# Magnitudes of every odd unit on ScalarE, the second layer one tick later, and x requested right behind its last reader

## The chip, the cores and the metric

The kernel runs on one core of a Trainium2 chip. Its engines are TensorE (PE, with its weight loads PEld), VectorE (DVE), ScalarE (ACT), GpSimd (POOL) and SyncE (SP, which here only issues DMAs). The metric is device time in microseconds (us) of one execution.

## The reference

Two stages follow each other. The attention has 4 batches of 12480 tokens with 128 channels and 32 inducing vectors; the second stage is a layer of width 2048 with a rational activation between its two matmuls.

```python
def mab(q, kv):
    s = scale * (q @ kv.transpose(0, 2, 1))
    s = s - s.max(-1, keepdims=True)
    a = np.exp(s)
    a /= a.sum(-1, keepdims=True) + 1e-09
    return a @ kv
h = mab(I, x)          # 32 inducing rows over all tokens of a batch
x = mab(x, h)          # every token over the 32 rows of h

h = x @ w_in           # (49920, 128) @ (128, 2048)
P = a[0] + a[1] * h + a[2] * h2 + a[3] * h3
Q = 1.0 + np.abs(b[0]) * np.abs(h) + np.abs(b[1]) * h2
g = P / (Q + 1e-06)
return (g @ w_out).astype(np.float32)
```

## The kernel before

**Units and ticks.** A batch is cut into 26 token tiles of 480 tokens. The first layer's 2048 columns are cut into 8 pairs of 128. One pair over one tile is a *unit*, with the key (b, n, q): batch, tile, and pair q from 0 to 7. There are 4 x 26 x 8 = 832 units, and a tile is eight of them. `fast_ticks` (line 894) issues one unit after the other, a *tick* each. Every engine takes its own instructions in the order in which they are written there, since the order is pinned. The engines run apart from each other and wait only for data and for buffers to come free.

**A unit's way.** `first` (838) makes the unit's 128x960 hidden values in PSUM with two f16 matmuls (`hp<-at,st`) a tick ahead; three such buffers `hp` exist. The unit's magnitudes `u` are taken one of two ways:

- A *plain* unit has `mask` (904) on VectorE, which reads `hp` and clears the sign bit (`DVE TENSOR_SCALAR u<-hp`). Then `moved` (853) adds a constant to `hp` with two further matmuls on TensorE (`hp<-same,by`), so they have to wait for the mask.
- A *shifted* unit has the constant already in `hp`, and one `Abs` with a bias on ScalarE (`ACT ACTIVATE u<-hp,all`) undoes it on the way. It needs no `moved`.

`shifted` (778) says which is which: of the odd q, 1, 3 and 7 are shifted and 5 is plain, and the even q are all plain. One tick later VectorE makes `l` of `u` and `hp` (`l<-u,all,hp`), which releases `hp`. Two units share one tile of `u`, and ScalarE turns each such pair with one `Ln` and, four ticks on, one `Sigmoid` (128x1920 each; a table load stands ahead of each run of four). Thirteen ticks behind a unit's first tick (`BEHIND`), in odd ticks, VectorE finishes the even unit of a pair (`l<-l,all,u`) and POOL the odd one with two instructions (`last_on_pool`, 952). `second` (858) then multiplies by `w_out` and adds up the 16 column blocks of a tile in `po`, of which there is one buffer. It comes fourteen ticks behind the unit.

**The end of a tile.** With q = 7, `second` adds two bf16 matmuls (`po<-at,st`), and the tile's sums are then complete. The next call of `fetch` (879) copies them with VectorE (`oT<-po`) and requests the write to `out` on SP. That call is the one in `side` (789), at the end of the same tick. A tick whose `second` has q = 0 is called *late*: its `second` stands at the tick's end, since it needs `po` to be copied away. Fourteen ticks behind, the tile's end falls into the tick of the unit q = 5, and the late tick is that of q = 6. The engines' order at that place is

```
tick q=5  PE:  second(q=7) first half, first(q=6), second(q=7) second half, bf16 pair, moved(q=5)
          DVE: finish, mask(q=5), l of q=4, side: copy of po
tick q=6  PE:  first(q=7), moved(q=6), side, second(q=0)
          DVE: mask(q=6), l of q=5, side
```

**Attention as side work.** `side` hands out pieces of the attention to the ticks, by budgets for TensorE, VectorE and POOL. `ahead` (740) works on the next batch: `pass1` (375) scores it against the inducing vectors, `pooled` (446) adds its values up, then the new first-layer weights are made. `attend` (767) works on the batch at hand: `pass3` (651) scores tokens against the 32 rows of `HT`, and `spread` (723) sends the results to the tiles `at` with four small DMAs per 480 tokens. The last batch has no `ahead`.

**How x comes in.** All DMAs stand in SP's one queue, in program order: x by columns for `pass1` (`xTa<-x_c`) and `pass3` (`xTb<-x_c`), x by rows for `pooled` (`x<-x_t`, with a POOL memset beside it), the `at<-hl` pieces and the `out<-oT` writes. Each kind of x has four buffers, a block of 480 tokens in each. `columns` (333) requests block n + 4 when block n + 1 is taken, and `pooled` requests block n + 3 ahead of the matmuls of block n. Blocks are used in groups of four, so the fourth block of a group is requested in the step that uses it. `landed` (327) holds a group back until three ticks after the request of its fourth block, if that request is already made.

Of the kernel before, what the change touches and what calls it, by code (L numbers as in the profile page):

```python
# [21 lines left out]
M = 32  # L22
C = 128
HB = 4
BT = HB * TP
# [167 lines left out]
class Kernel:  # L193
# [138 lines left out]

    def columns(self, b, kind):

        ts = [self.x_columns(b, n, kind) for n in range(4)]

        def turns():
            for n in range(self.NB):
                yield ts.pop(0)
                if n + 4 < self.NB:  # L340
                    ts.append(self.x_columns(b, n + 4, kind))

        return turns()

    def wide_columns(self, b):

# [28 lines left out]
    def pass1(self, b):  # L375

        nc, ap = self.nc, self.ap
        X = mybir.AxisListType.X
        e = ap.tile([P, self.NG, BT], F32, tag="e", name=f"e{b}")
        mxs = ap.tile([P, self.NG, 2], F32, tag="mxs", name=f"mxs{b}")  # L380
        nc.gpsimd.memset(mxs, -3.0e38)
        xs = self.wide_columns(b) if self.boot else self.cols.pop((b, "a"))
        for g in range(self.NG):
            nb = min(4, self.NB - 4 * g)
            yield from self.landed("a", b, g)
            yield "pe", 1.0
            pc = self.misc(f"pc{b}_{g}")
            for j in range(nb):
                nc.tensor.matmul(pc[M * j:M * j + M, 0:BT], self.ind, next(xs), start=True, stop=True)
            rows = slice(0, M * nb)  # L390
            for i in range(2):
                yield "v", 0.36
                c = slice(BT // 2 * i, BT // 2 * (i + 1))
                nc.vector.tensor_scalar(out=e[rows, g, c], in0=pc[rows, c], scalar1=1.0, scalar2=None, op0=ALU.mult, op1=ALU.max, accum_out=mxs[rows, g, i:i + 1])
            self.free()
        if self.boot:
            self.wide_rows(b)
        else:
            self.xs[b] = [self.x_rows(b, n) for n in range(4)]
        yield "v", 0.1  # L400
        mx = ap.tile([P, 1], F32, tag="mx", name=f"mx{b}")
        nc.vector.tensor_reduce(out=mx, in_=mxs.rearrange("p g i -> p (g i)"), axis=X, op=ALU.max)
        yield "pe", 0.2
        pm = self.misc(f"pm{b}")
        nc.tensor.transpose(out=pm[0:1, 0:P], in_=mx, identity=self.ident)
        yield "v", 0.3
        mt = ap.tile([1, 1, M], F32, tag="mt", name=f"mt{b}")
        nc.vector.tensor_reduce(out=mt[:, 0], in_=pm[0:1, 0:P].rearrange("o (j m) -> o m j", m=M), axis=X, op=ALU.max)
        self.free()
        nm = ap.tile([1, 4, M], F32, tag="H", name=f"nm{b}")  # L410
        nc.vector.tensor_scalar(out=nm, in0=mt.broadcast_to((1, 4, M)), scalar1=-1.0 / math.sqrt(C), scalar2=None, op0=ALU.mult)
        yield "pe", 0.2
        pb = self.misc(f"pb{b}")
        nc.tensor.matmul(pb[:, 0:4], nm.rearrange("o j m -> o (j m)"), self.ones, start=True, stop=True)
        yield "v", 0.1
        nmc = ap.tile([P, 1], F32, tag="nmc", name=f"nmc{b}")
        nc.vector.tensor_copy(out=nmc, in_=pb[:, 0:1])
        self.free()
        self.e[b] = e
        self.exps.append(lambda: self.exp_rows(b, e, nmc))  # L420
        self.flush()
# [24 lines left out]
    def pooled(self, b, own=None):  # L446

        nc, ap = self.nc, self.ap
        e = self.e[b]
        acc = ap.tile([P, C + 1], F32, tag="acc", name=f"acc{b}")  # L450
        xs = self.xs.pop(b)

        def turned(g):
            rows = slice(0, M * min(4, self.NB - 4 * g))
            for c in range(HB):
                yield "pe", 0.22
                if c == 0:
                    pt = self.misc(f"pt{b}_{g}").rearrange("p (c n) -> p c n", c=HB)
                nc.tensor.transpose(out=pt[0:TP, c, rows], in_=e[rows, g, TP * c:TP * c + TP], identity=self.ident[rows, rows])
            eT = ap.tile([TP, HB, P], F32, tag="eT", name=f"eT{b}_{g}", bufs=2)  # L460
            yield from self.act(lambda: nc.scalar.activation(eT[:, :, rows], pt[0:TP, :, rows], AF.Identity, bias=0.0, scale=1.0))
            eTs.append(eT)

        eTs, early = [], int(self.boot)
        while self.e_done.get(b, 0) < self.NG:
            self.flush()
            yield "wait", 0
        if early:
            yield from turned(0)
        for g in range(self.NG):  # L470
            nb = min(4, self.NB - 4 * g)
            if g + early < self.NG:
                yield from turned(g + early)
            eT = eTs.pop(0)
            self.free()
            yield from self.landed("x", b, g)
            for k in range(HB * nb):
                j, c = divmod(k, HB)
                if c == 0:
                    yield "pe", 0.4  # L480
                if k == 0:
                    ph = self.misc(f"ph{b}_{g}")
                if c == 0 and self.boot and (4 * g + j) % 3 == 0 and g + j:
                    self.xs[b] = xs
                    self.wide_rows(b)
                elif c == 0 and not self.boot and 0 < 4 * g + j < self.NB - 3:
                    xs.append(self.x_rows(b, 4 * g + j + 3))
                nc.tensor.matmul(ph[M * c:M * c + M, 0:C + 1], eT[:, c, M * j:M * j + M], xs[4 * g + j][:, c, :], start=(j == 0), stop=(j == nb - 1))
            yield "v", 0.2
            if g == 0:  # L490
                nc.vector.tensor_copy(out=acc, in_=ph[:, 0:C + 1])
            else:
                nc.vector.tensor_tensor(out=acc, in0=ph[:, 0:C + 1], in1=acc, op=ALU.add)
            self.free()
        yield "pe", 0.3
        pq = self.misc(f"pq{b}")
        nc.tensor.matmul(pq[0:M, 0:C + 1], self.fold, acc, start=True, stop=True)
        yield "v", 0.4
        rs = ap.tile([M, 1], F32, tag="rs", name=f"rs{b}")
        nc.vector.tensor_scalar(out=rs, in0=pq[0:M, C:C + 1], scalar1=1e-9, scalar2=None, op0=ALU.add)  # L500
        nc.vector.reciprocal(out=rs, in_=rs)
        yield "v", 0.2
        H = ap.tile([M, C], F32, tag="H", name=f"H{b}")
        nc.vector.tensor_scalar(out=H, in0=pq[0:M, 0:C], scalar1=rs, scalar2=None, op0=ALU.mult)
        self.free()
        yield "pe", 0.3
        pt = self.misc(f"HT{b}")
        nc.tensor.matmul(pt[:, 0:4 * M], H, self.ident4.rearrange("p a m -> p (a m)"), start=True, stop=True)
        yield "v", 0.2
        while own is None and self.scored < b - 2:  # L510
            yield "wait", 0
        HT = own if own is not None else ap.tile([C, 4 * M], F32, tag="HT", name=f"HT{b}", bufs=2)
        nc.vector.tensor_copy(out=HT, in_=pt[:, 0:4 * M])
        self.free()
        self.HT[b] = HT
# [135 lines left out]
    def pass3(self, b, groups):  # L651
# [4 lines left out]
        for fours in groups:  # L656
            wide = ap.tile([TP, 2, HB, 4, M], F32, tag="a", name=f"a{b}_{fours[0]}")
            todo = []
            for i, r in enumerate(fours):
# [3 lines left out]
                for j in range(HB * nb):  # L663
# [1 line left out]
                    if j == 0:  # L665
                        pc = self.misc(f"pd{b}_{r}")
                    if j % HB == 0:
                        xT = next(self.cols[b, "b"])
                    nc.tensor.matmul(pc[0:TP, M * j:M * j + M], xT[:, TP * (j % HB):TP * (j % HB) + TP], self.HT[b][:, 0:M], start=True, stop=True)
                a = wide[:, i, :, 0:nb]  # L670
                sc = pc[0:TP, 0:HB * nb * M].rearrange("p (j c m) -> p j c m", m=M, c=HB)
                yield "v", 0.7
# [104 lines left out]

    def shifted(self, q):

        return self.fast and q % 2 == 1 and q != 5  # L780

    def step(self, which):

# [110 lines left out]
    def fast_ticks(self, units):  # L894
# [10 lines left out]
            V.tensor_scalar(out=u.u.bitcast(I32), in0=u.h.bitcast(I32), scalar1=0x7FFFFFFF, scalar2=None, op0=ALU.bitwise_and)  # L905

        self.first(units[0])
        for t in range(n + BEHIND + 2):
            u, last, d, done = at(t), at(t - 1), at(t - BEHIND), at(t - BEHIND - 1)
            group, turn = divmod(t - TURNS - 2, 2 * TURNS)  # L910
            w = at(2 * TURNS * group + 2 * (turn % TURNS))
            late = done and done.key[2] == 0
# [6 lines left out]
            if u:  # L919
                if t % 2 == 0:  # L920
                    u.pair = self.mp.tile([P, 2, 2, BT], F32, tag="u", name=f"u{u.i}", bufs=self.rooms["u"])
                    u.u = u.pair[:, 0]
                    mask(u)
                    if late:
                        self.fetched = self.fetch()
                else:
                    u.u = last.pair[:, 1]
                    if not plain(u):
                        A.activation(u.u, u.h, AF.Abs, bias=p.z_back, scale=1.0)
            if t % 2 and d:  # L930
                V.scalar_tensor_tensor(out=d.g, in0=d.g, scalar=p.z_k3, in1=d.u, op0=ALU.add, op1=ALU.mult)
                self.last_on_pool(at(t - BEHIND + 1), d)
# [11 lines left out]
                A.activation(w.pair, w.pair, AF.Sigmoid, bias=p.lnc, scale=-2.0)  # L944
            self.side(u or units[-1])
            if late:
                if not u:
                    self.fetch()
                self.second(done)
        self.fetch()  # L950

# [123 lines left out]
                self.again()  # L1075


class Unit:


# [26 lines left out]
```

## Time and profile before

| | |
|---|---|
| median of 3 runs | 2566.98 us (2561.35 to 2567.44) |
| the profiled execution, its own time | 2566.77 us |
| its span, first to last instruction | 2564.9 us |
| TensorE (PE) busy | 2285.1 us, 89% |
| VectorE (DVE) busy | 2269.3 us, 88% |
| ScalarE (ACT) busy | 2149.7 us, 84% |
| POOL busy | 1445.7 us, 56% |
| mean granted TensorE clock | 0.956 of 2.4 GHz |

The three engines that carry the units are all near nine tenths busy, but the shares are means over a stretch with much side work and one with little. 188.8 us pass ahead of the first copy of a finished tile, and the ticks of the tiles counted 0 to 61 lie beside the side work of two kinds until 1699.1 us. The remaining 42 tiles lie beside score passes alone. Matmul ends are modelled in these records, so start-to-start distances are used where they can be. An instruction's line is in most cases that of a helper (L177), so it is found by its tiles.

### The profile page before, as it was taken

To read this page: it belongs to the slowest core of one execution; us is meant where nothing else is said; L and a number is where in the kernel's file an instruction comes from. 1 tells how busy PE (TensorE), PEld (TensorE's weight loads), DVE (VectorE), ACT (ScalarE), POOL (GpSimd) and SP (SyncE) were. 2 spreads that over 40 slices of the span, in tenths; PEclk is the share of its full clock that TensorE was granted. 3 is DMA by queue.
4 is the path that set the end of the run, shared out by engine and by line. 5 is a ranking of instruction groups with operands and counts; after the bars stand their busy time and mean duration, and the time that the engine had idled before them with its cause. 6 is when DMAs were issued, how large, how long until landed. Compare 5 with 4: busy or idle time off the path is not lost.

```text
span 2564.9 us, 25969 instructions
## 1 busy us (share of the span) xinstructions
PE 2285.1 (89%) x8670; PEld 1112.6 (43%) x8670; DVE 2269.3 (88%) x2490; ACT 2149.7 (84%) x1487; POOL 1445.7 (56%) x997
## 2 busy tenths in 40 slices
PE   4479999899899899999889989999999999999997
PEld 2244444444434444444434434444444444444443
DVE  2688899889998988988798879999999999999995
ACT  1177899888888998988799968889989899999995
POOL 0325566555555565665465546565656566666666
PEclk6579999999999999999999989999999999999999
DMA  9113201310132012002211220001010100000000
GB/s 251 53 31 115 64 26 31 78 50 20 58 100 62 18 52 66 28 27 89 81 35 35 70 58 27 12 20 43 24 43 23 44 18 30 18 18 20 16 16 17
DMA packets 117112, 121.03 MB, mean 47 GB/s; under 512 B 13289, under 2 KB 115561, under 8 KB 116969
## 3 DMA queue, kind: packets, MB, share of 16 engines
q1 hardware_dynamic: 116969, 119.28, 16.4%
q8 instruction: 70, 1.15, 0.2%
q14 instruction: 73, 0.60, 0.1%
HBM read 80.89 MB, written 25.56 MB: 42 GB/s over the span
## 4 chain that ended last, share of the span: by engine, by line
PE 44%; DVE 33%; issue 11%; ACT 6%; DMA 3%; POOL 2%; SPq 1%; DVEq 0%; POOLq 0%; ACTq 0%
PE po L177 27%; DVE l L177 15%; DVE u L177 12%; PE hp L177 10%; ACT u L177 4%; PE pd L177 3%; DVE oT L177 2%; ACT L177 1%; DVE asm L177 1%; PE pc L177 1%; SPq L177 1%; POOL u L177 1%; DMA xw<-x_t 1%; DMA xTw<-x_c 1%; DVE cv L177 1%
## 5 line engine op out<-in xcount | busy, mean ns | idle before, releaser
L177 PE MATMUL po<-l,w_out 128*128 128x480 f32 x3328 | 1579.4, 580 | 9.0 <-POOL l L177 8.1
L177 DVE SCALAR_TENSOR_TENSOR l<-u,all,hp 128x960 f32<-128x960 f32 x832 | 1002.2, 1205 | 32.8 <-PE hp L177 21.8
L177 POOL TENSOR_SCALAR u<-l,all 128x960 f32<-128x960 f32 x416 | 447.3, 1075 | 958.9 <-DVE l L177 838.7
L177 POOL TENSOR_TENSOR l<-u 128x960 f32<-128x960 f32 x416 | 927.0, 2228 | 34.6
L177 PEld LDWEIGHTS po<-l,w_out 128*128 128x128 f32 x3328 | 628.9, 193 | 380.9 <-issue 213.2
L177 ACT ACTIVATE u<-u,all 128x1920 f32<-128x1920 f32 x416 | 765.3, 1887 | 1.2
L177 ACT ACTIVATE u<-u 128x1920 f32<-128x1920 f32 x416 | 737.5, 1797 | 5.6 <-DVE l L177 4.5
L177 DVE TENSOR_SCALAR u<-hp 128x960 int32<-128x960 int32 x520 | 597.2, 1148 | 99.1 <-PE hp L177 97.2
L177 ACT ACTIVATE u<-hp,all 128x960 f32<-128x960 f32 x312 | 328.0, 1051 | 263.2 <-PE hp L177 257.3
L177 DVE SCALAR_TENSOR_TENSOR l<-l,all,u 128x960 f32<-128x960 f32 x416 | 521.1, 1253 | 2.4 <-ACT u L177 2.4
L177 PE MATMUL hp<-at,st 128*128 128x480 f16 x1664 | 481.0, 371 | 21.3 <-DVE l L177 17.5
L177 PE MATMUL hp<-same,by 96*128 96x480 f16 x1040 | 302.3, 372 | 140.0 <-DVE u L177 134.0
L177 PEld LDWEIGHTS <-st 128*128 128x128 f16 x1872 | 183.0, 99 | 490.1 <-issue 475.1
L177 ACT ACT_TABLE_LOAD x235 | 301.5, 1283 | 4.8 <-PEq L1100 0.7
L177 PEld LDWEIGHTS <-by 96*128 96x128 f16 x1040 | 102.6, 99 | 369.9 <-issue 333.4
L177 DVE COPY oT<-po 128x480 f32<-128x480 f32 x104 | 67.8, 651 | 61.3 <-PE po L177 61.1
L177 PEld LDWEIGHTS pd<-HT,xTb 128*120 128x120 f32 x832 | 101.9, 195 | 17.0 <-issue 9.7
L177 PE MATMUL pd<-HT,xTb 128*120 128x32 f32 x832 | 98.7, 274 | 3.9 <-DMA xTb<-x_c 3.8
L177 PE MATMUL po<-at,st 128*128 128x480 f16 x208 | 59.1, 366 | 0.0
L177 DVE TENSOR_SCALAR_CACHE_REDUCE e<-pc 128x240 f32<-128x240 f32 (+1 forms) x56 | 21.1, 401 | 31.9 <-PE pc L177 31.9
L177 ACT ACTIVATE a<-a 120x512 f32<-120x512 f32 (+2 forms) x21 | 14.9, 728 | 41.1 <-DVE a L177 41.0
L177 PE MATMUL ph<-x,eT 120*32 120x129 f32 x624 | 25.6, 292 | 24.0 <-DMA x<-x_t 14.0
(110 smaller groups left out, 609.4 us busy)
## 6 DMA issues: line engine op xcount, KB each, us to landing
xTb<-x_c SPq DMA_DIRECT2D x104, 240.0 KB, 2.8
out<-oT SPq DMA_DIRECT2D x104, 240.0 KB, 2.0
xTa<-x_c SPq DMA_DIRECT2D x78, 240.0 KB, 3.0
x<-x_t SPq DMA_DIRECT2D x78, 240.0 KB, 4.0
at<-hl SPq DMA_DIRECT2D x416, 30.0 KB, 1.8
xw<-x_t SPq DMA_DIRECT2D x8, 720.0 KB, 13.1
xTw<-x_c SPq DMA_DIRECT2D x5, 960.0 KB, 12.4
raw<-w_in SPq DMA_DIRECT2D x4, 480.0 KB, 10.3
```

What stands on the lines that cost most here:

```text
L177: ins = call(*args, **kw)
```

## The change

Four edits are made together.

- `shifted` loses its exception: q = 5 is shifted too. In 104 units a mask on VectorE and two `moved` matmuls on TensorE go, and an `Abs` on ScalarE comes.
- `second` and what follows it come fifteen ticks behind a unit. The end of a tile falls into the tick of q = 6, and the late tick is that of q = 7. VectorE's and POOL's last steps stay thirteen ticks behind.
- The call of `fetch` in a late tick stands behind both branches, since late ticks are odd now. The call in `side` still comes first in all but the first ticks.
- The class `Blocks` replaces the generator of `columns`. Its `read`, called right behind the last matmul that reads a block, requests the next block. `pooled` does the same for x by rows: block n + 4 behind the last matmul of block n, with its memset. For the first batch's wide tiles nothing changes.

```diff
     def columns(self, b, kind):
-        ts = [self.x_columns(b, n, kind) for n in range(4)]
-        def turns():
-            for n in range(self.NB):
-                yield ts.pop(0)
-                if n + 4 < self.NB:
-                    ts.append(self.x_columns(b, n + 4, kind))
-        return turns()
+        return Blocks([self.x_columns(b, n, kind) for n in range(4)], (self.x_columns(b, n, kind) for n in range(4, self.NB)))
...
-                nc.tensor.matmul(pc[M * j:M * j + M, 0:BT], self.ind, next(xs), start=True, stop=True)
+                nc.tensor.matmul(pc[M * j:M * j + M, 0:BT], self.ind, xs.take(), start=True, stop=True)
+                xs.read()
...
-                elif c == 0 and not self.boot and 0 < 4 * g + j < self.NB - 3:
-                    xs.append(self.x_rows(b, 4 * g + j + 3))
                 nc.tensor.matmul(ph[M * c:M * c + M, 0:C + 1], eT[:, c, M * j:M * j + M], xs[4 * g + j][:, c, :], start=(j == 0), stop=(j == nb - 1))
+                if c == HB - 1 and not self.boot and 4 * g + j + 4 < self.NB:
+                    xs.append(self.x_rows(b, 4 * g + j + 4))
...
-                        xT = next(self.cols[b, "b"])
+                        xT = self.cols[b, "b"].take()
...
+                    if j % HB == HB - 1:
+                        self.cols[b, "b"].read()
...
     def shifted(self, q):
-        return self.fast and q % 2 == 1 and q != 5
+        return self.fast and q % 2 == 1
...
-        for t in range(n + BEHIND + 2):
-            u, last, d, done = at(t), at(t - 1), at(t - BEHIND), at(t - BEHIND - 1)
+        for t in range(n + BEHIND + 3):
+            u, last, d, done = at(t), at(t - 1), at(t - BEHIND), at(t - BEHIND - 2)
...
-                    if late:
-                        self.fetched = self.fetch()
...
+            if late:
+                self.fetched = self.fetch()
...
             if late:
-                if not u:
-                    self.fetch()
                 self.second(done)
...
+class Blocks:
+    def __init__(self, held, more, ahead=True):
+        self.held, self.more, self.ahead = held, more, ahead
+    def take(self):
+        return self.held.pop(0) if self.held else next(self.more)
+    def read(self):
+        if self.ahead:
+            self.held += [t for t in [next(self.more, None)] if t is not None]
```

## Rows read from the trace of the kernel before

**Rows 1.** Busy time of the engines by stage: ahead of the first finished tile's copy, tiles 0 to 61, and from there to near the end. Columns: stretch and its length, then each engine's busy time with its instructions, the granted TensorE clock, the DMA share and rate.

```profile
0.00:188.80 188.80, 104.19 (x551) 57.88 (x552) 111.82 (x296) 60.77 (x57) 38.58 (x57) 0.66 0.45 113
188.80:1699.10 1510.30, 1384.03 (x5468) 673.91 (x5467) 1344.05 (x1437) 1292.71 (x896) 858.27 (x608) 0.97 0.18 52
1699.10:2541.50 842.40, 782.79 (x2618) 374.83 (x2617) 808.70 (x755) 796.26 (x535) 536.79 (x328) 1.00 0.08 25
```

**Rows 2.** The same view of one tile without side work and of one with a score pass (32 `pd` matmuls) beside it, in the order PE, PEld, DVE, ACT, POOL.

```profile
2301.16:2321.08 19.92, 18.85 (x61) 8.79 (x60) 19.75 (x19) 19.66 (x14) 13.19 (x9) 1.00 0.03 12
649.50:673.80 24.30, 22.70 (x96) 12.37 (x95) 22.06 (x23) 18.98 (x13) 11.96 (x8) 1.00 0.21 62
```

**Rows 3.** The timeline around the end of that tile without side work: start, duration, engine, operation, in brackets the idle time before it and what ended it.

```profile
2300.35 0.57 PE L177 MATMUL po<-at,st 128*128 128x480 f16 x2
2300.75 0.57 PE L177 MATMUL hp<-same,by 96*128 96x480 f16 x2
...
2301.16 0.64 DVE L177 COPY oT<-po 128x480 f32<-128x480 f32 x1
2301.29 0.56 PE L177 MATMUL hp<-at,st 128*128 128x480 f16 x2
...
2301.73 1.14 DVE L177 TENSOR_SCALAR u<-hp 128x960 int32<-128x960 int32 x1
...
2302.79 1.20 DVE L177 SCALAR_TENSOR_TENSOR l<-u,all,hp 128x960 f32<-128x960 f32 x1
2302.92 0.56 PE L177 MATMUL hp<-same,by 96*128 96x480 f16 x2 [1.07 <-DVE u L177]
...
2303.32 2.58 PE L177 MATMUL po<-l,w_out 128*128 128x480 f32 x6
...
2303.79 1.05 ACT L177 ACTIVATE u<-hp,all 128x960 f32<-128x960 f32 x1
...
2304.73 3.48 ACT L177 ACTIVATE u<-u 128x1920 f32<-128x1920 f32 x2
```

**Rows 4.** The costliest groups, of which these are the mask, the `Abs` and the `moved` matmuls: busy time, mean ns of one, then idle time of the engine just before them and what ended it.

```profile
L177 DVE TENSOR_SCALAR u<-hp 128x960 int32<-128x960 int32 x520 | 597.2, 1148 | 99.1 <-PE hp L177 97.2
L177 ACT ACTIVATE u<-hp,all 128x960 f32<-128x960 f32 x312 | 328.0, 1051 | 263.2 <-PE hp L177 257.3
L177 PE MATMUL hp<-same,by 96*128 96x480 f16 x1040 | 302.3, 372 | 140.0 <-DVE u L177 134.0
```

**Rows 5.** Who waited for whom between 188.8 and 1699.1 us: sum in us, times, longest.

```profile
ACT u L177 <- PE hp L177: 203.5, 96, 12.2
...
PE hp L177 <- DVE u L177: 73.2, 70, 3.6
...
PE ph L177 <- DMA x<-x_t: 14.0, 3, 9.6
...
PE pc L177 <- DMA xTa<-x_c: 10.7, 2, 7.7
...
PE ph L177 <- POOL x L177: 10.0, 8, 2.3
...
PE po L177 <- POOL l L177: 2.6, 6, 0.7
```

**Rows 6.** The timeline of SP's queue (SPq) and of TensorE around the longest wait of TensorE for x.

```profile
1519.87 0.37 SPq L177 DMA_DIRECT2D out<-oT  x1
1520.64 4.94 SPq L177 DMA_DIRECT2D at<-hl  x8
1525.69 1.58 SPq L177 DMA_DIRECT2D x<-x_t  x3
...
1529.64 0.66 PE L177 MATMUL ph<-x,eT 120*32 120x129 f32 x8 [9.57 <-DMA x<-x_t]
```

**Rows 7.** Busy time by stretch where ScalarE has next to no idle time, among tiles 0 to 61: 5, 4 and 3 tiles, in the order PE, PEld, DVE, ACT, POOL.

```profile
339.80:456.30 116.50, 106.16 (x427) 52.23 (x427) 107.56 (x109) 111.39 (x81) 70.40 (x51) 0.99 0.13 37
827.10:915.00 87.90, 79.30 (x248) 36.56 (x248) 80.41 (x78) 84.95 (x61) 54.73 (x35) 0.98 0.05 17
1333.30:1401.40 68.10, 62.28 (x216) 30.70 (x215) 59.85 (x56) 67.21 (x48) 41.72 (x25) 0.97 0.11 33
```

**Rows 8.** Busy time by stretch behind 1699.1 us: the first, third, fifth, seventh and last stretch have 4, 2, 4, 6 and 16 tiles with little side work, the others 1, 2, 2 and 2 tiles with a score pass.

```profile
1699.10:1779.60 80.50, 76.09 (x244) 35.42 (x244) 79.57 (x74) 78.14 (x54) 52.68 (x33) 1.00 0.10 31
1779.60:1807.40 27.80, 24.31 (x93) 12.92 (x92) 23.52 (x24) 22.47 (x16) 14.20 (x10) 0.94 0.12 37
1807.40:1847.30 39.90, 37.62 (x120) 17.58 (x120) 39.56 (x38) 38.23 (x27) 26.42 (x17) 1.00 0.06 19
1847.30:1894.90 47.60, 44.90 (x189) 24.68 (x188) 42.62 (x43) 41.86 (x29) 26.34 (x17) 1.00 0.20 57
1894.90:1979.30 84.40, 76.95 (x244) 35.34 (x244) 83.60 (x81) 79.88 (x55) 54.76 (x35) 1.00 0.06 18
1979.30:2026.90 47.60, 44.90 (x189) 24.69 (x188) 42.63 (x43) 41.58 (x29) 26.36 (x17) 1.00 0.20 58
2026.90:2151.40 124.50, 114.35 (x364) 53.02 (x364) 123.12 (x116) 119.11 (x81) 81.09 (x51) 1.00 0.06 18
2151.40:2197.20 45.80, 43.13 (x174) 23.00 (x172) 42.00 (x42) 41.48 (x29) 26.36 (x17) 1.00 0.11 33
2197.20:2521.40 324.20, 303.72 (x969) 141.13 (x968) 320.60 (x297) 316.23 (x213) 212.63 (x131) 1.00 0.06 18
```

More of the change, by code (lines that the diff above doesn't have):

```diff
@@ L381, in pass1 @@
         nc.gpsimd.memset(mxs, -3.0e38)
-        xs = self.wide_columns(b) if self.boot else self.cols.pop((b, "a"))
+        xs = Blocks([], self.wide_columns(b), ahead=False) if self.boot else self.cols.pop((b, "a"))
         for g in range(self.NG):
```

## The prediction

> **What bounds the kernel now.** I read the stages first, then a single tile, then the waits.
>
> By stage [rows 1], the first 188.8 us are a start that the change hardly touches. Then 62 tiles take 1510.3 us, 24.4 us each, with the attention of the next batch beside them. There TensorE is idle for 1510.3 - 1384.0 = 126 us, VectorE for 166 us and ScalarE for 218 us. No engine is full, so these tiles are held by waits between the engines, with TensorE the nearest to full. Behind 1699.1 us all is tighter: ScalarE is busy for 796 of 842 us, VectorE for 809.
>
> A tile without side work [rows 2] shows why. In its 19.92 us VectorE is busy for 19.75 and ScalarE for 19.66, while TensorE needs 18.85. VectorE paces it and ScalarE has 0.26 us to spare. A tile with a score pass beside it takes 24.30 us, with TensorE busy for 22.70, VectorE for 22.06 and ScalarE for 18.98: TensorE paces that one, and ScalarE has 5.3 us to spare.
>
> The timeline at a tile's end [rows 3] shows where TensorE loses its time. The bf16 pair ends the sums (its issue is over at 2300.75, where `moved` of q = 5 begins). The copy begins at 2301.16, the mask of q = 6 stands behind the copy in VectorE's queue (2301.73), and `moved` of q = 6 can't begin until that mask is done: TensorE waits 1.07 us. This is one wait a tile, and it is the form of the 73.2 us that `hp` waits for VectorE's `u` among tiles 0 to 61 [rows 5]. The rest of TensorE's idle time there that has a name is 14.0 + 10.7 us for x, 10.0 us for POOL's memset of x, and 2.6 us for POOL's half of `l` [rows 5]. ScalarE's idle time there is nearly all for `hp`, 203.5 us: ScalarE is behind TensorE there, it doesn't hold it.
>
> **The change part by part.**
>
> *Magnitudes of q = 5.* By start-to-start distances [rows 3] a mask takes VectorE 2302.79 - 2301.73 = 1.06 us, a pair of `moved` matmuls takes TensorE 2303.32 - 2302.92 = 0.40 us, and an `Abs` takes ScalarE 2304.73 - 2303.79 = 0.94 us. The durations [rows 4] are 1148 and 1051 ns, each with an overlap at its end. So each tile gives VectorE 1.06 us and TensorE 0.40 us back, and ScalarE gets 0.94 us more. Over 104 tiles that is 110, 42 and 98 us. None of the three is the sum by itself: it depends on who paces the tile.
>
> Where there is no side work ScalarE becomes the pace: 19.66 + 0.94 = 20.60 us against 19.92, so +0.7 a tile. VectorE falls to 18.7 and TensorE to 18.5 us, and I see nothing that ScalarE would then wait for. Behind 1699.1 us [rows 8] the 32 tiles of the quiet stretches take 653.5 us now, with ScalarE busy for 631.6. With 32 x 0.94 = 30.1 more that is 661.7, so +8 us if all of ScalarE's 21.9 us of idle time can be filled, and +30 if none can. It sits beside the score passes, with nothing that forbids filling it, so I take +12. The 7 tiles with a score pass have 168.8 - 157.2 = 11.6 us of idle TensorE and gain something like those of the earlier batches, with an end at 7 x 0.4 + 11.6 = 14 us; but ScalarE there rises to 147.4 + 6.6 = 154 us, so I take -6. The late tiles give **+6**, between -6 and +30.
>
> Among tiles 0 to 61 there are 12 in which ScalarE is as good as full [rows 7], with the softmax and its table loads: 272.5 us, of which ScalarE is busy for 263.6. With 12 x 0.94 = 11.3 that is 274.8: **+2**. In the other 50 ScalarE has some 200 us to spare for 47 us of work, and the `moved` pairs that go, 50 x 0.40, give **-20** on the engine that paces most of them.
>
> A rule of the Trainium skill speaks against this edit. "ScalarE: Activation LUTs", section "Rules for kernel authors", says that simple elementwise operations belong on VectorE and not on ScalarE. The rows differ for this one: on these 128x960 f32 values out of PSUM the `Abs` is the shorter of the two [rows 4]. By the rule the edit would load the wrong engine, and the rival on ScalarE's pace below would be the likeliest, with its 2615 us.
>
> *The tile's end a tick later.* The end now falls into the tick of q = 6, and that unit's mask stands ahead of the copy instead of behind it. So `moved` of q = 6 needs nothing of the copy, and the 1.07 us go. What is late next is the copy itself, since `second` of q = 0 wants `po`. From the bf16 pair's end to the copy's end it is 2301.80 - 2300.75 = 1.05 us [rows 3], and TensorE has `moved` and `first` meanwhile, 0.40 us each. So some 0.3 us of waiting come back a tile, less where side work lies between: over 50 tiles **+15**, and nothing at best. Of the 73.2 us [rows 5] some 13 belong to the 12 full tiles. Of the other 60 some lie behind longer side work on VectorE (the longest is 3.6 us, where the tile's end alone makes 1.07), which stays, so I take two thirds: **-39**, between 0 and -60. POOL's result has three ticks on its way instead of two, which ends the 2.6 us. The values `l` are held a tick longer, in sixteen buffers for fifteen ticks, so VectorE may still run a tick ahead of TensorE, which is more than it does. The last tick that is added issues only multiplications whose data POOL brings anyway: 0.
>
> *x behind its last reader.* The longest wait of TensorE [rows 6] shows what it mends. Three requests of x stand behind a write of `out` and eight `at` pieces, which hold SP from 1520.64 to 1525.58. Then x lands, and TensorE has waited 9.57 us for the fourth block of a group. The fourth block was requested in the step that uses it; now it is requested at the end of the group before, some ticks earlier and ahead of those pieces. Of the 24.7 us [rows 5] I take **-20**, between 0 and -25. The memsets of x are moved up in POOL's queue as well, right behind the matmuls that free the buffer. POOL may stand there until TensorE gets to them, and its half of `l` stands behind, but that is wanted ticks later and POOL is busy for 858 of 1510 us [rows 1]. With its 10.0 and 2.6 us I take **-6**, between +5 and -13. SP too may now stand at a request until TensorE has read the block, with `at` and `out` behind it: by the place of the requests that is the same tick, so 0. The hold of three ticks on a group now takes effect, and can move side work by a tick or two: 0, for that work is done well before it is needed (that for the fourth batch is over at 1699.1 us [rows 1], behind tile 61, and its first tile is number 78).
>
> *The sum.* +6 + 2 - 20 + 15 - 39 - 20 - 6 = -62. The profiled execution took 2566.77 us with a span of 2564.9, and the median is 2566.98, so there is nothing to convert: 2566.8 - 62 = **2505 us**.
>
> **The rivals.**
>
> *The wait only moves.* The copy comes late because VectorE must first do `l` of q = 5, which now needs an `Abs` that ScalarE does behind an activation of some 1.7 us (3.48 us for two [rows 3]). Then `second` of q = 0 waits as long as `moved` did. For it speaks that `po` has one buffer; against it the 0.80 us of work in between and ScalarE's idle time [rows 5]. The 39 us are not gained: 2505 + 39 = 2544 us.
>
> *ScalarE sets the pace everywhere (the slower side).* Between two `Abs` ScalarE has such activations, and VectorE stands at `l` until the `Abs` has come, with `hp` unreleased and TensorE behind it. If that already holds tiles of 24 us, each of the 50 takes 0.94 more and TensorE's gains turn to idle time: 47 + 2 + 12 + 7 - 20 for x gives 2615 us. It ends slower as soon as tiles 0 to 61 gain less than the late tiles lose, some 12 us. For it speaks the tile without side work; against it 203.5 us in which ScalarE waits for TensorE.
>
> *The requests don't help.* SP's queue is held by something else at the new place, a reader that TensorE has not reached, and x comes as late: -20 and -6 fall away, 2531 us.
>
> **How the numbers follow.** Forecast 0.55, for 2475 to 2540 us. The wait only moves 0.13; the requests don't help 0.10; both of these with dearer late tiles, within 0.3%, 0.06; ScalarE's pace 0.10; and 0.06 for a larger gain, when all of TensorE's named waits go: -20 - 60 - 25 - 13 + 2 - 6 = -122, 2445 us. A difference of 0.3%, 7.7 us, is about what a measurement of this kernel can tell from no change. Faster by more than that: 0.55 + 0.13 + 0.10 + 0.06 = 0.84; within it 0.06; slower 0.10. The range leaves out ScalarE's pace and most of the larger gain, and reaches up to no change: 2470 to 2565 us.
>
> **What the profile after would show.** Right: 416 masks, 416 `Abs` and 832 `moved` matmuls; quiet tiles behind 1700 us at 20.6 us with ScalarE without idle time; the waits of `hp` for `u` down to some 20 us among tiles 0 to 61; no wait of TensorE for `x` or `xTa` of several us; and 62 tiles in some 1445 us. Wrong: quiet tiles much over 20.7 us; TensorE waiting for the copy by 1 us a tile; VectorE's `l` waiting for ScalarE's `u` by tens of us among tiles 0 to 61.

## The result and the profile after

The changed kernel takes 2432.98 us (median of 4 runs, 2431.8 to 2437.1) against 2564.16 us before: the ratio is 0.9495, with a 95% interval of 0.9469 to 0.9521. That is 131 us less, where 62 were forecast, and it lies under the range. The profiled execution took 2437.1 us with a span of 2435.3; both are some 130 us less than in the kernel before.

The first view of after is the busy time by stage, which answers to [rows 1]: the start, tiles 0 to 61, and tiles 62 to 101. The columns are the same: the stretch, its length, PE, PEld, DVE, ACT, POOL, the granted clock.

```profile
0.00:195.50 195.50, 105.52 (x548) 57.91 (x549) 110.65 (x295) 64.84 (x62) 40.08 (x57) 0.66 0.46 110
195.50:1575.70 1380.20, 1326.08 (x5282) 645.30 (x5280) 1274.63 (x1358) 1343.43 (x957) 862.40 (x606) 0.99 0.20 56
1575.70:2411.20 835.50, 795.76 (x2602) 370.64 (x2601) 767.93 (x731) 826.16 (x573) 534.09 (x329) 0.99 0.08 25
```

Tiles 0 to 61 go from 1510.3 to 1380.2 us, so by this split all of the gain lies there. TensorE's idle time falls from 126 to 54 us, and its busy time by 58, of which the matmuls that went make 25. ScalarE is busy for 1343 of 1380 us, and TensorE for 1326. The granted clock of that stage rises from 0.97 to 0.99. From tile 62 to tile 100's end the time goes from 822.4 to 818.3 us. The first copy of a finished tile comes 6.7 us later, one tick of which is the edit itself.

The two stages don't hold quite the same work. Making the fourth batch's first-layer weights, 70 matmuls that keep TensorE busy for some 9 us, began 71.5 us ahead of tile 62's copy and now begins 0.6 us ahead of it. So some 8 us of TensorE's work have left tiles 0 to 61, and the late tiles got it: for like work the early tiles gained less than these figures say, and the late ones more.

The second view is who waited for whom among tiles 0 to 61, the answer to [rows 5]; each line has the sum in us, the times, and the longest.

```profile
DVE l L177 <- ACT u L177: 53.1, 48, 3.4
...
PE hp L177 <- DVE l L177: 25.2, 38, 2.7
PE hp L177 <- DVE u L177: 22.1, 21, 2.7
ACT u L177 <- PE hp L177: 21.4, 24, 2.4
PEld po L177 <- DVE oT L177: 16.1, 38, 0.5
```

The waits for x, its memset and POOL's `l` are gone from TensorE's matmuls. The wait for the mask is down from 73.2 to 22.1 us. ScalarE waited 203.5 us for `hp` and now waits 21.4; VectorE waits for ScalarE instead, 53.1 us, and TensorE for VectorE's `l`, 25.2 (8.7 before).

The third view is the timeline at the end of a quiet tile, the answer to [rows 3].

```profile
2187.15 0.57 PE L177 MATMUL po<-at,st 128*128 128x480 f16 x2
2187.55 0.57 PE L177 MATMUL hp<-same,by 96*128 96x480 f16 x2
...
2188.07 0.65 DVE L177 COPY oT<-po 128x480 f32<-128x480 f32 x1
2188.20 0.56 PE L177 MATMUL hp<-at,st 128*128 128x480 f16 x2
...
2188.77 0.30 PEld L177 LDWEIGHTS po<-l,w_out 128*128 128x128 f32 x2 [0.47 <-DVE oT L177]
2188.77 2.28 PE L177 MATMUL po<-l,w_out 128*128 128x480 f32 x5
```

`moved` of q = 6 follows the bf16 pair directly. The copy runs beside it and `first`, and `second` of q = 0 begins 0.17 us after `first` has been issued (0.40 us from 2188.20): that is what is left of the 1.07 us. The weight load ahead of it shows the wait for the copy.

### The profile page after: what moved, and what is told of

The parts are those of the page before. It is cut to its first block, busy times and chain, and to the rows that moved or that the text cites. A ratio compares the mean times of both kernels' runs of the same rounds, so it can differ in the third digit from the quotient of the medians.

```text
span 2435.3 us, 25780 instructions
## 1 busy us (share of the span) xinstructions
PE 2241.4 (92%) x8462; PEld 1079.8 (44%) x8462; DVE 2160.0 (89%) x2386; ACT 2235.6 (92%) x1590; POOL 1450.1 (60%) x997
## 4 chain that ended last, share of the span: by engine, by line
PE 37%; ACT 31%; DVE 16%; issue 10%; SPq 2%; DMA 2%; POOL 1%; DVEq 0%; POOLq 0%; ACTq 0%
ACT u L177 25%; PE po L177 22%; PE hp L177 9%; DVE l L177 8%; ACT L177 5%; DVE u L177 3%; PE pd L177 3%; SPq L177 2%; DMA xTw<-x_c 1%; DVE cv L177 1%; DVE asm L177 1%; PE pgt L177 1%; PE pl L177 1%; DMA at<-hl 1%; POOL l L177 1%
## 5 line engine op out<-in xcount | busy, mean ns | idle before, releaser
L177 PEld LDWEIGHTS po<-l,w_out 128*128 128x128 f32 x3328 | 619.0, 192 | 385.8 <-issue 220.0
L177 ACT ACTIVATE u<-u,all 128x1920 f32<-128x1920 f32 x416 | 775.4, 1888 | 1.2
L177 DVE SCALAR_TENSOR_TENSOR l<-l,all,u 128x960 f32<-128x960 f32 x416 | 529.5, 1273 | 4.8 <-ACT u L177 4.8
L177 DVE TENSOR_SCALAR u<-hp 128x960 int32<-128x960 int32 x416 | 477.2, 1147 | 27.8 <-PE hp L177 26.1
L177 ACT ACTIVATE u<-hp,all 128x960 f32<-128x960 f32 x416 | 435.1, 1046 | 50.5 <-PE hp L177 46.4
L177 PEld LDWEIGHTS <-st 128*128 128x128 f16 (+1 forms) x1872 | 182.5, 98 | 554.6 <-issue 538.5
L177 PE MATMUL hp<-same,by 96*128 96x480 f16 x832 | 239.3, 368 | 48.1 <-DVE u L177 41.7
L177 PEld LDWEIGHTS <-by 96*128 96x128 f16 x832 | 82.0, 99 | 239.1 <-issue 211.7
L177 ACT ACTIVATE e<-e,nmc 128x960 f32<-128x960 f32 (+1 forms) x16 | 15.6, 993 | 32.9 <-DVE nmc L177 32.8
L177 PE MATMUL pa<-ident,a 120*128 120x120 f32 (+1 forms) x112 | 17.4, 281 | 28.8 <-DVE a L177 25.0
## 6 DMA issues: line engine op xcount, KB each, us to landing
xTw<-x_c SPq DMA_DIRECT2D x5, 960.0 KB, 12.6
```

The lines of the kernel that those rows point to most:

```text
L177: ins = call(*args, **kw)
```

## The experiments

Two theories were set against each other. By the first, each wait of TensorE is paid twice, by itself and by a stretch at half clock behind it. By the second, engine load sets the pace, and waits cover for each other. This table collects the profiled executions; "lost" is the time times the share of clock not granted, summed over the trace's clock records, and "idle" is the idle time before TensorE's matmuls.

| kernel | time against before | tiles 0-61, us | idle | lost | tiles 62-100, us |
|---|---|---|---|---|---|
| before | 1 | 1510.3 | 125.7 | 42.7 | 822.4 |
| x requests alone | 0.9806 | 1439.4 | 95.0 | 13.7 | 842.5 |
| tile's end alone | 0.9863 | 1489.0 | 106.3 | 37.5 | 804.1 |
| q = 5 alone | 0.9955 | 1493.8 | 148.7 | 29.0 | 823.1 |
| tile's end and q = 5 | 0.9802 | 1466.1 | 107.3 | 41.0 | 812.7 |
| tile's end and x | 0.9534 | 1400.7 | 54.2 | 13.7 | 812.2 |
| all three (after) | 0.9495 | 1380.2 | 53.8 | 15.4 | 818.3 |

The column "lost" is of one execution each, and it moves from one to the next. In the 35 runs of the kernel before beside the experiments, on three chips, the granted clock goes from 0.956, as in the profiled execution, to 0.969. On the chip of the first four experiments the medians over the runs are 0.962 before, 0.964 with x alone, 0.9585 with the tile's end alone, 0.9635 with q = 5 alone and 0.9565 with these two together. Within a chip, over the 35 runs, 0.01 of granted clock, which is 26 us of clock, goes with 11 us of time, a loose tie (correlation -0.6). By that estimate less than half of a loss shows as time.

In the rows with x, the work on the fourth batch's weights falls behind tile 61, as in the full change.

**The requests of x alone.** The edits of `columns`, `pass1`, `pooled`, `pass3` and `Blocks`, nothing else.

> The kernel before with the requests of x alone moved. Theory 1 (waits of TensorE are paid twice, by themselves and by the half clock granted behind them): the named waits for x and its memset among tiles 0 to 61, 14.0 + 10.7 + 2.5 + 10.0 = 37 us, go, and with them some 15 us lost at half clock: 2564 - 52 = 2512 us, and clock lost among these tiles falls from 43 us to under 30. Theory 2 (engine load sets the pace, waits are partly cover for each other): 2564 - 25 = 2539 us, clock lost as before.

It took 2515.56 us against 2564.43, a ratio of 0.9806 (0.978 to 0.9833), so 49 us less where the first theory had 52 and the second 25. Among tiles 0 to 61 TensorE's matmuls show no wait for x or its memset any more, and the clock loss fell to 13.7 us in the profile, below what was expected; by the medians over the runs it is only some 7 us less than before. Where the tiles are counted, the gain shows as 71 us early and 20 us more late: the work on the weights now falls behind tile 61, and the clock lost there goes from 1.7 to 10.2 us.

**The tile's end alone.** The loop of `fast_ticks` as in the change, `shifted` as before.

```diff
-            u, last, d, done = at(t), at(t - 1), at(t - BEHIND), at(t - BEHIND - 1)
+            u, last, d, done = at(t), at(t - 1), at(t - BEHIND), at(t - BEHIND - 2)
...
```

> The kernel before with the second layer fifteen ticks behind alone; q = 5 stays plain. Theory 1: of the 73.7 us that the matmuls of the added constant wait for the mask among tiles 0 to 61 some 50 go, and some 12 us at half clock: 2564 - 60 = 2504 us; quiet tiles go from 19.92 to about 19.75 us, paced by VectorE. Theory 2 (the wait only moves to the copy, the gain needs the lighter VectorE): 2564 - 10 = 2554 us.

It took 2528.58 us, 0.9863 (0.9837 to 0.9889): 36 us less, between the two. The wait for the mask among tiles 0 to 61 fell from 73.2 to 30.7 us, as the first theory has it, and the quiet tiles take 19.73 us. But the waits for x grew, as these lines of the same stretch show against [rows 5], and the clock loss hardly changed.

```profile
PE hp L177 <- DVE u L177: 30.7, 34, 2.4
PE pc L177 <- DMA xTa<-x_c: 22.1, 6, 7.6
...
PE ph L177 <- POOL x L177: 13.0, 7, 4.9
PE ph L177 <- DMA x<-x_t: 12.3, 2, 8.8
```

**The magnitudes of q = 5 alone.**

```diff
-        return self.fast and q % 2 == 1 and q != 5
+        return self.fast and q % 2 == 1
```

> The kernel before with q = 5 shifted alone; second layer fourteen ticks behind. Theory 1: the mask of q = 6 still stands behind the copy, and the matmuls of the added constant of q = 6 wait 0.4 us longer a tile since those of q = 5 no longer lie between: 110 instead of 74 us of that wait, so TensorE gains nothing, and ScalarE paces the quiet tiles at 20.6: 2564 to 2585 us. Theory 2 (load): 2564 - 45 = 2519 us.

It took 2552.49 us, 0.9955 (0.9937 to 0.9972). The wait for the mask rose as expected, though only from 73.2 to 86.7 us, and the late tiles gained nothing (823.1 us). But tiles 0 to 61 got 16 us shorter where no gain was expected, so the first theory's figure falls here. Its mechanism holds: TensorE's idle time rose by 23 us, nearly the 25 us of `moved` matmuls that went. In the two profiles the 16 us are about what the clock gave back, 13.7 us; by the medians over the runs the clock gave less, so where the 12 us come from stays open. It isn't the 45 us of the second theory either. The waits for x stayed as they were, 38 us with the line of `pd` (2.2):

```profile
PE ph L177 <- DMA x<-x_t: 14.9, 4, 9.3
...
PE pc L177 <- DMA xTa<-x_c: 11.3, 2, 8.2
PE ph L177 <- POOL x L177: 9.7, 7, 2.3
```

**The change without the requests of x.** The loop of `fast_ticks` and `shifted` of the change, x as before.

> The changed kernel with the requests of x as before. Theory 1: the waits for x come back with their half clock, 2433 + 50 = 2483 us. Theory 2: 2433 + 25 = 2458 us. If ScalarE by now paces nearly all tiles and fills its queue ahead of such a wait, part of it is hidden: 2433 + 35.

It took 2513.25 us, 0.9802 (0.9776 to 0.9827). So beside the other two edits the requests of x are worth 80 us, far above all three expectations, where alone they are worth 49. Alone, the tile's end gives 36 and q = 5 gives 12, and together 51: these two add up. It is x that is worth more beside them, and the tile's end is what makes it so: those two edits together, the run with q = 5 plain further down, give 0.9534, some 120 us, where alone they give 85. The waits show part of it:

```profile
PE pc L177 <- DMA xTa<-x_c: 22.7, 6, 7.7
PE ph L177 <- POOL x L177: 16.2, 7, 4.9
...
PE ph L177 <- DMA x<-x_t: 12.0, 2, 8.6
...
PE pd L177 <- DMA xTb<-x_c: 4.0, 3, 2.1
```

That is 55 us of waits for x where the kernel before has 37 (2.4 of it for `pd`), with 41 us lost to the clock where the full change has 15. By the table, 53.5 us of TensorE's idle time and 25.6 us of clock make 79 of the 86 us between their tiles 0 to 61, and the work on the weights that moved behind them is about the rest. Against x alone, 15 of the 31 us more lie in these tiles (86 for 71) and 14 behind them (6 us more for 20). Two further lines have the place of the longest of them, first SP's queue, then TensorE:

```profile
1214.92 4.95 SPq L177 DMA_DIRECT2D at<-hl  x8
1219.91 1.53 SPq L177 DMA_DIRECT2D xTa<-x_c  x3
...
1222.86 1.81 PE L177 MATMUL pc<-xTa,ind 128*32 128x480 f32 x2 [7.71 <-DMA xTa<-x_c]
```

It is the same picture as [rows 6]: eight `at` pieces ahead of the requests. The longer waits don't come of shorter ticks. With q = 5 alone the tiles take 24.1 us and the waits for x are 38 us; with the tile's end alone the tiles take 24.0 us and the waits are 51. So they came with the tile's end. In that run `pc` waits six times instead of twice, and five of the six, as one of the two before, look alike in the trace: a write of `out`, the last three or four requests of `xTa` right behind it, and TensorE waiting 2.6 to 3.6 us for them. Why more groups are used at that place was not taken apart.

**Filling the wait.** To see the clock by itself, the waits of the kernel before were left in place and TensorE was given useless work in them: matmuls by zeros, added onto the hidden values of q = 7.

```diff
+            if late and at(t + 1) and self.B * self.NB - 42 > u.key[0] * self.NB + u.key[1]:
+                for _ in range(2):
+                    for k in range(2):
+                        self.nc.tensor.matmul(at(t + 1).h[:, k], self.zero, self.same, start=False, stop=True, skip_group_check=True)
...
```

> The kernel before with 0.8 us of extra matmuls by zeros on TensorE between the first layer of q = 7 and the added constant of q = 6, in the 62 tiles with the attention of the next batch beside them: TensorE does them in a wait that it has there anyway. If the half clock behind such waits costs time of its own, fewer stretches at half clock follow: clock lost among these tiles from 43 us to about 28, and 2564 - 12 = 2552 us although TensorE has 50 us more to do. If only the waits cost, 2564 to 2580 us.

It took 2560.71 us, a ratio of 0.9975 (0.9958 to 0.9991): faster, by some 6 us, half of what the first theory had, with 0.8 us of added matmuls in each of 62 tiles. The stage view has tiles 0 to 61 and the rest:

```profile
187.50:1686.90 1499.40, 1407.15 (x5708) 687.58 (x5707) 1343.84 (x1437) 1293.18 (x897) 858.68 (x608) 0.99 0.18 52
1686.90:2510.80 823.90, 767.61 (x2580) 368.28 (x2580) 797.23 (x747) 778.98 (x524) 520.84 (x320) 1.00 0.08 25
```

VectorE, ScalarE and POOL have the same work as in [rows 1] to within 1 us. TensorE has 240 matmuls more, some 49 us, yet the tiles take 10.9 us less. The matmuls filled 34 us of waiting:

```profile
PE hp L177 <- DVE u L177: 38.8, 65, 2.8
```

The rest of what they cost is more than paid by the granted clock, which goes from 0.97 to 0.99: 5 stretches at 1.2 GHz instead of 20, with 17 instead of 43 us lost. This pair of profiles shows more than the runs do on the whole: their median clock goes from 0.959 to 0.966, which is 18 us less lost. So short waits of TensorE can have a price beyond themselves. The Trainium skill, "TensorE: Matmul & The Clock Gate", Part 1, "What's actually happening", says that the clock is set by how busy the array has been recently, and the 20 and 5 stretches agree.

**ScalarE's pace.** One `Sigmoid` in four of the changed kernel does half of its columns.

```diff
-                A.activation(w.pair, w.pair, AF.Sigmoid, bias=p.lnc, scale=-2.0)
+                part = w.pair[:, 0:1] if w.key[2] == 4 else w.pair
+                A.activation(part, part, AF.Sigmoid, bias=p.lnc, scale=-2.0)
```

> The changed kernel with one Sigmoid in four, that of the pair q = 4 and 5, done on half of its columns, the other half left as it is: ScalarE has 0.80 us less to do in each tile, nothing else changes. If ScalarE by now paces nearly all tiles, 90 of 104, also those beside the attention: 2433 - 72 = 2361 us. If TensorE still paces those and ScalarE only the quiet ones: 2433 - 25 = 2408 us.

2394.09 us, 0.9326 (0.9307 to 0.9345): against the change's 0.9495 that is some 40 us less for 83 us of ScalarE's work, between the two expectations. The stages say where:

```profile
190.20:1553.60 1363.40, 1320.33 (x5281) 645.22 (x5280) 1275.44 (x1357) 1297.65 (x958) 862.60 (x606) 0.99 0.20 57
1553.60:2345.20 791.60, 768.91 (x2568) 364.01 (x2567) 757.97 (x724) 778.47 (x563) 522.76 (x321) 1.00 0.08 26
```

The 39 late tiles got 26.7 of their 31 us, so ScalarE sets their pace. The 62 early tiles got 16.8 of 50: there TensorE, busy for 1320 of 1363 us, comes next as soon as ScalarE is relieved.

**The change with q = 5 plain.**

> The changed kernel with q = 5 plain again: what the magnitudes of q = 5 on ScalarE are worth beside the other two edits. Quiet tiles 19.73 us instead of 20.55, which is 20 us less; the tiles beside the attention have 1.06 us more on VectorE and 0.40 on TensorE each. If ScalarE has the pace there too, those gain little by the edit: 2433 + 10 = 2443 us. If VectorE and TensorE have it: 2433 + 45 = 2478 us.

2449.14 us, 0.9534 (0.9513 to 0.9554). Beside the other two edits the magnitudes of q = 5 are worth 0.4%, some 10 us; the two kernels were not timed together, and against the second timing of the change, below, it is 14. By the profiles it is 20 us in tiles 0 to 61, where VectorE and TensorE are relieved, less 6 us in the late ones, where ScalarE has the pace.

**q = 5 plain in the fourth batch alone.** That split by stage suggests to make the choice by batch.

```diff
-    def shifted(self, q):
-        return self.fast and q % 2 == 1
+    def shifted(self, b, q):
+        return self.fast and q % 2 == 1 and (q != 5 or b < self.B - 1)
...
```

> The changed kernel with q = 5 plain in the fourth batch alone, which has no next batch's attention beside it: 26 tiles go from ScalarE's pace to VectorE's, 19.73 instead of 20.55 us in the quiet ones, of which there are some 18, and less in those with a score pass: 2433 - 16 = 2417 us. If the pace there is not ScalarE's, 2433 us or more.

2426.34 us, 0.9449 (0.9432 to 0.9467). It was then timed again, beside the changed kernel and beside a third version with q = 5 plain in the last two batches.

> The changed kernel once more, beside the two versions that follow, on one chip: 0.950 of the time before.

> The version with q = 5 plain in the fourth batch alone, once more: 0.945 of the time before, 12 us under the changed kernel, if the first comparison holds.

> The changed kernel with q = 5 plain in the third and fourth batch. Some 8 quiet tiles of the third batch gain 0.8 us each, but its first 12 tiles, beside the next batch's attention, have 1.06 us more on VectorE and 0.40 on TensorE. If TensorE and VectorE have the pace in those: nothing over the version with the fourth batch alone, 0.945 to 0.948. If ScalarE has it there: 0.942.

On one chip, with 2570.18 us before, the changed kernel took 2436.73 us (0.9478, 0.9463 to 0.9493), the version with the fourth batch plain 2424.9 us (0.9433, 0.9418 to 0.9448), and the one with two batches plain 2433.11 us (0.9465, 0.9449 to 0.9481). The runs of the first two do not overlap: 2433.59 to 2438.39 and 2423.0 to 2426.96. So the fourth batch alone gains 12 us, where 16 were expected at first, and beats both kernels. The third batch gives 8 of them back, by the profiles 5 to 6 us in tiles 0 to 61, beside the attention, and some 4 us behind them. A quiet tile of the fourth batch then takes 19.7 us, with VectorE busy throughout:

```profile
2365.50:2385.20 19.70, 19.04 (x62) 8.62 (x59) 19.70 (x19) 19.64 (x14) 13.20 (x8) 1.00 0.04 14
```

## Why the prediction was wrong

The direction and the mechanism of each edit were right. The step that failed is the sum for tiles 0 to 61, -68 us where -130 were measured. The waits for the mask and for x were taken too small, the copy's wait was charged with +15 us and shows before no matmul of TensorE, and two terms stood at nothing: the clock, and the side work that moves.

| term, tiles 0 to 61 | forecast | measured in the profiles |
|---|---|---|
| `moved` matmuls that go | -20 | 122 matmuls in 61 pairs of 0.40 us: -24 |
| wait of `moved` for the mask | -39 | 73.2 to 22.1: -51 |
| wait of `second` for the copy | +15 | none before matmuls; 16.1 us before weight loads |
| waits for x, the memset, POOL's `l` | -26 | 14.0 + 10.7 + 2.4 + 10.0 + 2.6, all to nothing: -40 |
| the clock | not in the sum | 42.7 to 15.4 us lost: -27 |
| ScalarE's pace | +2 | `hp` waiting for VectorE's `l`, 8.7 to 25.2: +17 |
| side work that moves | 0 | the fourth batch's weights, now behind tile 61: -8 |
| sum | -68 | -133, where the profiles have -130 |

**The terms left out.** The granted clock of 0.97 stood in [rows 1] and was read past. Three per cent of 1510 us are 45 us of TensorE's time, on the engine that I had named as the nearest to full, and the waits that the change removes are what stands ahead of the slow stretches. The run with the filled waits shows that this loss is in part time, and not a mere sign of idleness, in a kernel that TensorE paces. But this pair of profiles makes the term large. By the medians over the runs on one chip the granted clock goes from 0.958 to 0.962, which is 15 us less lost over the whole execution, where the pair has 25. In the changed kernel it counts for less: its second profile lost 23.9 us instead of 15.4 and took 1381.6 us for the same tiles instead of 1380.2, since ScalarE is as full there. So the -27 is an account of TensorE's time; how much of it is elapsed time can't be read off it; by the estimate above it is less than half.

The other term at nothing was the hold on a group of x, which was to move side work by a tick or two. The work on the fourth batch's weights moved by some three tiles, 24 ticks; that the hold is the reason was not tested.

**The requests of x.** I took 20 of 24.7 us and 6 of 12.6. All of it went. The larger error is one of method: I priced the edit by the waits of the kernel before. The runs show that it is worth 49 us there and 80 us beside the other edits, and half of that difference lies in tiles 0 to 61, where the same requests cost 51 to 55 us of waits beside the tile's end instead of 37. The three edits alone give 49 + 36 + 12 = 97 us, and together 131.

**The tile's end.** The step was right in its mechanism. The copy's wait came back as forecast, in 38 tiles, but before the weight loads of `second`; in the quiet tile 0.17 us of it is left between the matmuls' starts, where I had taken 0.3. Two thirds of the mask's wait was a good share when the edit was alone (73.2 to 30.7) and is 70% beside the others.

**ScalarE in the quiet tiles.** 20.60 us were forecast; they take 20.55, with ScalarE busy throughout. The late tiles came out 4 us under instead of 6 us over, although the work on the weights moved into them. The 32 other tiles took 9 us more for the 12 forecast, and the seven tiles with a score pass gained 13 us instead of 6 (168.8 to 155.6 us). I had bounded them by 14, and chose the middle because ScalarE would come near there. It did, with 155.1 us busy of 155.6 in the four stretches of [rows 8], but what counted was that it was kept fed:

```profile
1662.70:1685.30 22.60, 21.98 (x91) 11.96 (x90) 20.72 (x24) 22.51 (x17) 13.15 (x9) 1.00 0.19 55
1726.20:1771.10 44.90, 44.39 (x184) 24.04 (x183) 40.48 (x41) 44.75 (x32) 26.66 (x17) 1.00 0.21 61
```

**The rivals.** That the wait only moves fell: TensorE's matmuls show no wait for the copy among tiles 0 to 61. That the requests don't help fell with the run on them alone. ScalarE's pace is real, but it came as the next limit and not as a loss: the 203.5 us of its waiting were there to be used. With it fell, for this operation on these operands, the rule of the Trainium skill that simple elementwise work (its row names relu, max, min, add and mul) belongs on VectorE ("ScalarE: Activation LUTs", Rules for kernel authors): the run with q = 5 plain is slower than the change by 10 to 14 us, in part for the `moved` matmuls that a plain unit needs. In the late tiles alone the rule's outcome holds, as the version by batch shows.

**The range.** Its lower end went to the named waits of before and no further, and the larger gain had 0.06. The bound of -122 that I had worked out for it was too near: it had no term for the clock or for side work that moves, and it assumed that gains add up.

## What to carry to other kernels

Read the granted clock of each stage as a term of the sum, over several runs: where TensorE paces, a short wait that an edit removes may give back time at half clock as well. An edit can be worth more beside another than alone: the requests of x gave 49 us alone and 80 beside the tile's end, which had brought further waits for x. Before a gain is laid to a stage, see whether work has crossed its border. Request a buffer's next load right behind its last reader, ahead of whatever else will be put on the same queue. Where stages have different limits, make the choice between two engines by stage: here the same move gained 20 us in one and lost 6 in the other.

## What the runs showed of the hardware

The granted clock fell to 1.2 GHz behind short waits of TensorE, not only behind the long ones. Of the 20 falls among tiles 0 to 61 of the kernel before, 16 came close behind a wait of 1.0 to 2.6 us, and 4 at longer ones, three of them for x. But of 56 such short waits 40 stand ahead of no fall. With waits filled by useless matmuls, the 20 falls became 5 in the profiles, and over the runs the kernel got 0.25% faster with some 49 us more matmul work at full clock.
